# Two rows of w_out split earlier, products with m placed behind the newest half product, m made a step ahead, row writes moved behind m's loads

## The chip, the cores and the metric

The kernel runs on one core of a Trainium2 chip. Time is device microseconds for one execution. The core has TensorE (PE: matrix products; PEld: its weight loads), VectorE (DVE), ScalarE (ACT), GpSimd (POOL) and SyncE (SP), which here issues nearly all transfers. Each engine works through its own instructions in order, and waits at an instruction until what it needs is there.

## The reference

Eight batches of attention between 512 tokens and 32 states in 8 heads, and then a feed-forward block over all rows, whose weights are drawn as 64-bit floats. Below, a is the softmax of the scores over the states, and a2 the same with the states as the queries:

```python
def _attn_ref(x, state):          # x: 8 x 8 x 512 x 64, state: 8 x 8 x 32 x 64
    scores = scale * np.matmul(x, state.transpose(0, 1, 3, 2))
...
    xread = np.matmul(a, state)
...
    sread = np.matmul(a2, x)
    return np.concatenate([xread, sread], axis=2)

def _moe_ref(x, w_in, w_out):     # 4608 rows, w_in 512 x 2048, w_out 2048 x 512
    h = x @ w_in
    g = h - np.tanh(h)
    return g @ w_out
```

## The kernel before

**Chunks and rows.** The tokens of batch i are chunk i (512 rows); the states' rows of all batches are chunk 8 (256 rows). For chunks 0 to 7 the read of the state and the first weight are joined: xread @ w_in is a @ m, where m (256 x 2048 for each batch) is state times w_in, head by head. m is handled in quarters q of 512 columns, and each quarter in two halves k. A hidden product for row f (one of 16 groups of 128 columns of w_in) is `hps`, from `m` and `aT` (the transposed softmax); tanh on ScalarE and a subtraction on VectorE make g. An output product for row f is `ops`, from g and row f of w_out (`wo`), four of them, one for each 128 tokens, added up over the rows in four banks.

**Splitting.** A number is kept as two: a cast to fp32r on ScalarE (the high part) and a subtraction on VectorE (the low part), both in the helper at L103. A product is then three: high with high, high with low, low with high (L501 to L503, L556 to L558). For chunk 0's first half, eight rows (HALT = 8), g and w_out's rows 0 to 7 (PLAIN = 8) stay plain fp32 (tiles `wp`, two rows each) and one fp32 product is used (L499, L554). `split_row` splits those rows later, since the other chunks need them split (`wo`).

**Raw weights.** A block of 64-bit weights is loaded raw, and made fp32 in four steps: two on VectorE, one on ScalarE, one on VectorE (`Weight.steps`, L132 to L136). The raw tiles rotate through six buffers, so a load waits until the block six loads earlier is converted.

**m.** For batches 0 and 1 m is made by `m_first_two` as soon as two blocks of w_in are there (products `mps` at L181, then four copies on ScalarE by `free`). Batch 0's quarters 2 and 3 go to memory (`md02`, `md03`) and are loaded again (`mr02`, `mr03`) by `load_m`, which also splits them (`m02`, `m03`). `mr` is one buffer. For batches 2 to 7 `m_units` makes m from w_in read back and the split states (`sms`, `slr` split to `sls`), stores it (`md` from `st` and `sl`), and `load_m` loads it. Copies out of these banks follow each other in a fixed order, and a new product with m waits until the last of them is done (`behind_free`).

**The order of the work.** A loop over steps `st` goes through `order`: chunk 0's rows 0 to 7, chunk 1's 16 rows, chunk 0's rows 8 to 15, chunks 2 and 3. A step calls, in this order, conversions of weights (tables CONV and WO), `prepare` (which calls `load_m`) where a quarter begins and the hidden product for the row LAG = 2 steps ahead, `split_row` (table SPLITS), `m_first_two` (table PAIRS), side work of other batches, `keep_row` (table KEEP: two writes of a split row of w_out to memory, `wod`, on SyncE) and `mix_rows`, and at last the output products of its own row. A second loop handles chunks 4 to 7 in pairs with the rows read back from `wod` and `wsd`. What stands in which place on an engine is then set by a planner that lists the instructions by its own estimate of when each can start; `tc.issue_after(x)` tells it that what is made inside comes behind x. `keep_row` is told to come behind the last load of raw weights.

Of the kernel before, what the change touches and what calls it, by code (L numbers as in the profile page):

```python
# [27 lines left out]
LAG = 2  # L28
# [1 line left out]
EARLY_S = 2  # L30
LONE = 1
HALT = 8
PLAIN = 8
TURN = (0, 1, 3, 2)


# [1 line left out]
def attention_ffn(ctx: ExitStack, tc: tile.TileContext, xT, xn, bd, bh, sp, sm, sl, win, wout, xout, tout, sout):  # L38
# [10 lines left out]
    nc = tc.nc  # L49
# [28 lines left out]
    mdram = [  # L78
        [dram.tile([2, 4, NS, 512], F32, name=f"md{b}{q}") for q in range(NQ)]
        if b != 1  # L80
        else None
        for b in range(B)
    ]
# [61 lines left out]
    loadlog = []  # L145
# [10 lines left out]
    def second(q):  # L156
        return pool.tile([P, 2, 512], F32, tag="stage", name=f"mr1{q}", bufs=SB)

    def m_first_two(q, p):

        k = p // 2
        if p == 0:

            tag, bufs = ("m", MB) if q == 1 else ("mr", RRB)
            m_first[q] = pool.tile([P, 2, 512], F32, tag=tag, name=f"mr0{q}", bufs=bufs)
            m_second[q] = second(q)
        if p % 2 == 0:
            return
        pss = [bank(ps_a, f"mps0{q}{p - 1 + c}") for c in range(2)]
        run = []  # L170
        for b in range(2):
            for c in (1, 0):
                for e in range(2):
                    r = slice(64 * e, 64 * e + 64)
                    at = 64 * b + 32 * (e ^ c)
                    rows = slice(at, at + 32)
                    with ExitStack() as behind:
                        if run:
                            behind.enter_context(tc.issue_after(run[-1]))
                            behind.enter_context(tc.high_priority())  # L180
                        made = nc.tensor.matmul(  # L181
                            pss[c][rows], sps[r, p - 1 + c, rows], wfs[q, k][r, c], start=True, stop=True
                        )
                    if not run:
                        behind_free(made)
                    run.append(made.ins)
        for c in range(2):
            free(m_first[q][64 * c : 64 * c + 64, k], pss[c][0:64])
            free(m_second[q][64 * c : 64 * c + 64, k], pss[c][64:128])
        if q >= 2 and k:  # L190
            nc.sync.dma_start(mdram[0][q].rearrange("g h n f -> (h n) g f"), m_first[q])

    freed = [None]

    def free(out, src, **more):

# [11 lines left out]
    def m_units():  # L208
# [8 lines left out]
        for q in range(NQ):  # L217
            for k in range(2):
                w = pool.tile([P, 2, 512], F32, tag="wf", name=f"w1{q}{k}", bufs=WB)
                nc.sync.dma_start(w, wf[q][:, 2 * k : 2 * k + 2])  # L220
                for c in range(2):
# [32 lines left out]
                            nc.sync.dma_start(mdram[6 + j][q][k, 2 * c + e], late[rows])  # L254
                    yield

    def load_m(b, q):
        if b == 0 and q < 2:
            return [m_first[q][:, k] for k in range(2)], None
        if b == 1:  # L260
            r = m_second[q]
        else:
            r = pool.tile([P, 2, 512], F32, tag="mr", name=f"mr{b}{q}", bufs=RRB)
            nc.sync.dma_start(r, mdram[b][q].rearrange("g h n f -> (h n) g f"))
        m = pool.tile([P, 2, 2, 512], F32R, tag="m", name=f"m{b}{q}", bufs=MB)
        split(m[:, 0], m[:, 1], r)
        return [m[:, 0, k] for k in range(2)], [m[:, 1, k] for k in range(2)]
# [17 lines left out]
        return his, los  # L285

    def convert_wout(f, part):
        if f < PLAIN:
            if f % 2 == 0:
                plain[f // 2] = big(f"wp{f}", [P, 2, DM], F32)  # L290
            part.convert(plain[f // 2][:, f % 2])
            return
        w = pool.tile([P, 512], F32, tag="c2", name=f"wor{f}", bufs=CSB)
        part.convert(w)
        wo[f] = big(f"wo{f}", [P, 2, DM], F32R)
        split(wo[f][:, 0], wo[f][:, 1], w)


    plain = {}
# [177 lines left out]
    class Chunk:  # L477
# [11 lines left out]
        def hidden(self, f):  # L489

            i, n = self.i, self.n
            ps = bank(ps_h, f"hps{i}_{f}")[:, :n]
            cols = slice((f % 4) * P, (f % 4) * P + P)
            mhi, mlo = self.m[f // 4]
            ahi, alo = aTs[i][:, 0], aTs[i][:, 1]
            nk = 2 if i < B else 4
            for k in range(nk):
                if mlo is None:
                    nc.tensor.matmul(ps, mhi[k][:, cols], ats[k], start=(k == 0), stop=(k == 1))  # L499
                    continue  # L500
                nc.tensor.matmul(ps, mhi[k][:, cols], ahi[:, k], start=(k == 0), stop=False)  # L501
                nc.tensor.matmul(ps, mhi[k][:, cols], alo[:, k], start=False, stop=False)  # L502
                made = nc.tensor.matmul(ps, mlo[k][:, cols], ahi[:, k], start=False, stop=(k == nk - 1))  # L503
                if CL <= i < B:
                    chain[0] = made.ins
            self.finish(f, ps)

        def finish(self, f, ps):
            i, n = self.i, self.n
            t = pool.tile([P, 512], F32, tag="t", name=f"t{i}_{f}", bufs=TB)[:, :n]  # L510
            if CL <= i < B:
                if f % 4 < 2:
                    self.g[f // 4, f % 2] = big(f"G{i}_{f}", [P, 2, 512], F32)
                g = self.g[f // 4, f % 2][:, f % 4 // 2]
                main(nc.scalar.activation(t, ps, AF.Tanh), nc.vector.tensor_sub(g, ps, t))  # L515
                return
            if i == 0 and f < PLAIN:
                g = self.g[f] = pool.tile([P, 512], F32, tag="g", name=f"g{i}_{f}", bufs=GB)
                tanhs.append((nc.scalar.activation(t, ps, AF.Tanh).ins, nc.vector.tensor_sub(g, ps, t).ins))
                return  # L520
            tanhs.append((nc.scalar.activation(t, ps, AF.Tanh).ins, nc.vector.tensor_sub(t, ps, t).ins))  # L521
            g = pool.tile([P, 2, 512], F32R, tag="g", name=f"g{i}_{f}", bufs=GB)
            split(g[:, 0, :n], g[:, 1, :n], t)
            self.g[f] = g
# [23 lines left out]
        def add(self, f, t):  # L548
            g, o = self.g[f], self.o[t]
            tok = slice(t * P, t * P + P)  # L550
            stop = f + 1 in self.begins or f == NFF - 1
            if self.i == 0 and f < PLAIN:
                w = plain[f // 2][:, f % 2]
                return nc.tensor.matmul(o, g[:, tok], w, start=(f in self.begins), stop=stop).ins  # L554
            w = wo[f]
            nc.tensor.matmul(o, g[:, 0, tok], w[:, 0], start=(f in self.begins), stop=False)  # L556
            nc.tensor.matmul(o, g[:, 0, tok], w[:, 1], start=False, stop=False)  # L557
            return nc.tensor.matmul(o, g[:, 1, tok], w[:, 0], start=False, stop=stop).ins  # L558
# [44 lines left out]
    chunks = [Chunk(i) for i in range(B + 1)]  # L603
# [18 lines left out]
            nc.sync.dma_start(wf[q][:, p - 1 : p + 1], wfs[q, p // 2])  # L622


    CONV = [0, 0, 7, 8, 9, 10, 11, 12, 13, 14]
    WO = [0, 1, 2, 3, 4, 5, 6, 8, 9, 10, 12, 13, 14, 15, 16]
    SPLITS = [6 + x for x in range(PLAIN)]
    split_it = iter(range(PLAIN))
    PAIRS = [1, 1, 9, 9, 11, 11, 13, 13, 15, 15]
    rest = w0[1][2:] + w0[2] + w0[3]  # L630
    later = sorted([(s, 0, x) for s, x in zip(CONV, range(10))] + [(s, 1, x) for s, x in zip(WO, range(1, NFF))])
    loads = iter(w0[0] + wos[:1] + w0[1][:2] + [wos[x] if w else rest[x] for _, w, x in later])
# [168 lines left out]
    def keep_row(f):  # L801
        for half in range(2):
            cols = slice(256 * half, 256 * half + 256)
            with tc.issue_after(loadlog[-1]):
                nc.sync.dma_start(wod[:, f % 2, half, f // 2], wo[f][:, :, cols].bitcast(F32))

    def mix_rows(j):
# [38 lines left out]
    order = [(0, f) for f in range(HALT)] + [(1, f) for f in range(NFF)] + [(0, f) for f in range(HALT, NFF)]  # L846
    order += [(i, f) for i in range(2, CL) for f in range(NFF)]
    for st, (i, f) in enumerate(order):
            with ExitStack() as gates:
                for x in tanhs[st - 1] if st > 6 else (first,):  # L850
                    gates.enter_context(tc.issue_after(x))
                for _ in range(CONV.count(st)):
                    convert_win(*next(convs))
                    load(1)
                for _ in range(WO.count(st)):
                    x = next(wo_it)
                    convert_wout(x, wos[x])
                    load(1)
            if st + LAG < len(order):
                ni, nf = order[st + LAG]  # L860
                if nf % 4 == 0:
                    chunks[ni].prepare(nf // 4)
                chunks[ni].hidden(nf)
            with ExitStack() as gates:
                for x in tanhs[max(st - 1, 0)]:
                    gates.enter_context(tc.issue_after(x))
                for _ in range(SPLITS.count(st)):
                    split_row(next(split_it))
            if st in AHEAD:
                x = AHEAD.index(st)  # L870
# [145 lines left out]
    for n, duo in enumerate(duos):  # L1016
        a, b = duo.a.i, duo.b.i
# [5 lines left out]
        for s in range(8):  # L1023
            h = hs[per * s : per * s + per]
# [105 lines left out]
```

## Time and profile before

| what | value |
|---|---|
| median of 3 runs | 659.6 us (659.54 to 662.79) |
| the profiled execution | 660.7 us |
| its span, first to last instruction | 658.9 us |
| PE busy | 637.1 us, 97% |
| PEld, DVE, ACT busy | 485.7, 481.2, 383.3 us |
| DMA | 141.21 MB, mean 214 GB/s |
| granted TensorE clock, mean | 0.997 |

Busy times are sums over the whole span, and a matmul's end is modelled, so PE's 97% says that it rarely waits, not how well each product runs. Lines (L501 and so on) are those of the kernel before. In rows of the trace in order of time, the first number is the start, the second the length; what ended the idle time just before an instruction stands in square brackets. In rows of groups the count follows the x, then the busy time and the mean length in ns, then the idle time before them. A plain fp32 product leaves two records in the trace, a product of fp32r parts one. PEq, SPq and so on are an engine's issuing part.

### The profile page before, as it was taken

The page shows a single profiled execution, that of the slowest core. Times are in us where ns is not written, and L with a number is a line of the kernel's source. Part 1 is how long each engine was busy: PE and PEld are TensorE (multiplying, and loading weights), DVE is VectorE, ACT ScalarE, POOL GpSimd, SP SyncE. Part 2 cuts the span into 40 slices and gives each one's busy share as a digit, 9 for nine tenths or more (in the row PEclk, how much of TensorE's full clock was granted, in tenths as well). Part 3 has the DMA queues.
Part 4 walks back from the last instruction along what each step waited for, and adds up shares of the span by engine and source line. Part 5 has one row for each costly group of instructions (what it writes and reads, how often), then busy time and mean ns, then how long its engine had stood idle before and what let it go on. Part 6 is the DMA issues. An engine that isn't in the chain of part 4 may idle for free.

```text
span 658.9 us, 9567 instructions
## 1 busy us (share of the span) xinstructions
PE 637.1 (97%) x3442; PEld 485.7 (74%) x3442; DVE 481.2 (73%) x764; ACT 383.3 (58%) x666; POOL 26.9 (4%) x41
## 2 busy tenths in 40 slices
PE   5899899999999999999999999999999999999997
PEld 2434477767777778787878887778888888788996
DVE  5887799768557976799637886996965789754442
ACT  3755678667757576576655576355655553543532
POOL 2000000000000000000000000000000000343300
PEclk9899999999999999999999999999999999999999
DMA  9794489997978874644822446464565545899800
GB/s 316 247 366 156 165 289 340 345 320 240 284 243 269 277 254 167 222 161 164 287 96 100 159 125 213 143 203 131 156 186 188 162 129 181 296 324 347 279 8 32
DMA packets 67440, 141.21 MB, mean 214 GB/s; under 512 B 6977, under 2 KB 28737, under 8 KB 67393
## 3 DMA queue, kind: packets, MB, share of 16 engines
q1 hardware_dynamic: 64832, 132.21, 61.0%
q0 software_dynamic: 2560, 8.39, 3.6%
q8 instruction: 27, 0.44, 0.3%
q14 instruction: 21, 0.16, 0.1%
HBM read 96.01 MB, written 44.56 MB: 213 GB/s over the span
## 4 chain that ended last, share of the span: by engine, by line
PE 85%; DVE 8%; DMA 3%; ACT 2%; issue 1%; SPq 0%; ACTq 0%; DVEq 0%
PE X L965 12%; PE hps L501 9%; PE hps L502 9%; PE hps L503 8%; PE ops L556 8%; PE ops L558 8%; PE ops L557 8%; PE Y1m L965 5%; PE ops L554 4%; PE Y0m L965 4%; PE mps L235 2%; PE hps L499 2%; PE mls L242 2%; PE rps L447 1%; PE pps L426 1%
## 5 line engine op out<-in xcount | busy, mean ns | idle before, releaser
L501 PE MATMUL hps<-aT,m 128*128 128x512 f32 x240 | 95.9, 401 | 4.0 <-ACT aT L103 1.6
L502 PE MATMUL hps<-aT,m 128*128 128x512 f32 x240 | 94.0, 392 | 0.0
L503 PE MATMUL hps<-aT,m 128*128 128x512 f32 x240 | 93.4, 391 | 0.0
L556 PE MATMUL ops<-wo,g 128*128 128x512 f32 x224 | 87.3, 395 | 1.6 <-ACT g L103 1.6
L557 PE MATMUL ops<-wo,g 128*128 128x512 f32 x224 | 87.1, 391 | 0.0
L521 DVE TENSOR_TENSOR t<-hps,t 128x512 f32<-128x512 f32 (+1 forms) x72 | 45.1, 627 | 45.8 <-ACT t L521 45.5
L558 PE MATMUL ops<-wo,g 128*128 128x512 f32 x224 | 75.7, 394 | 0.0
L515 ACT ACTIVATE t<-hps 128x512 f32<-128x512 f32 x64 | 38.2, 597 | 63.8 <-PE hps L503 61.5
L515 DVE TENSOR_TENSOR G<-hps,t 128x512 f32<-128x512 f32 x64 | 43.9, 687 | 38.8 <-ACT t L515 38.7
L521 ACT ACTIVATE t<-hps 128x512 f32<-128x512 f32 (+1 forms) x72 | 39.6, 552 | 47.8 <-PE hps L503 46.4
L501 PEld LDWEIGHTS hps<-aT,m 128*128 128x128 f32 x240 | 44.9, 188 | 19.6 <-DVE G L515 3.2
L103 ACT CAST g<-t 128x512 fp32r<-128x512 f32 (+1 forms) x72 | 41.1, 574 | 25.6 <-DVE t L521 25.3
L103 DVE TENSOR_TENSOR g<-t,g 128x512 fp32r<-128x512 f32 (+1 forms) x72 | 45.1, 626 | 13.7 <-ACT g L103 13.4
L502 PEld LDWEIGHTS hps<-aT,m 128*128 128x128 f32 x240 | 45.1, 188 | 10.8 <-issue 1.7
L556 PEld LDWEIGHTS ops<-wo,g 128*128 128x128 f32 x224 | 41.9, 188 | 14.0 <-ACT g L103 2.0
L503 PEld LDWEIGHTS hps<-aT,m 128*128 128x128 f32 x240 | 45.1, 188 | 9.4
L558 PEld LDWEIGHTS ops<-wo,g 128*128 128x128 f32 x224 | 41.7, 188 | 11.5 <-issue 1.2
L557 PEld LDWEIGHTS ops<-wo,g 128*128 128x128 f32 x224 | 42.1, 188 | 9.2 <-issue 0.7
L965 PE MATMUL X<-g0m,W0m 128*128 128x512 f32 x192 | 46.9, 390 | 0.5 <-DVE g0m L103 0.5
L1003 POOL DMA_DIRECT2D wl<-wod x32 | 23.3, 729 | 587.5 <-DVE g1m L103 555.1
L965 PE MATMUL X<-g1m,W1m 128*128 128x512 f32 x192 | 45.9, 391 | 0.6 <-DVE g1m L103 0.6
L103 ACT CAST g1m<-G 128x1024 fp32r<-128x1024 f32 x28 | 29.3, 1055 | 28.8 <-PE Y1m L965 12.7
(262 smaller groups left out, 1182.0 us busy)
## 6 DMA issues: line engine op xcount, KB each, us to landing
mr<-md SPq DMA_DIRECT2D x26, 512.0 KB, 3.9
xT<-in_xT SPq DMA_DIRECT2D x16, 512.0 KB, 4.9
wod<-wo SPq DMA_DIRECT2D x32, 256.0 KB, 5.3
md<-st SPq DMA_DIRECT2D x64, 128.0 KB, 3.1
xn<-in_xn SPq DMA_DIRECT2D x16, 512.0 KB, 5.0
wsd<-ws SPq DMA_DIRECT2D x16, 512.0 KB, 3.5
W0m<-wsd SPq DMA_DIRECT2D x16, 512.0 KB, 4.0
W1m<-wsd SPq DMA_DIRECT2D x16, 512.0 KB, 4.3
```

The source lines that it names most:

```text
L103: return nc.scalar.copy(hi, src), (sub or nc.vector).tensor_sub(lo, src, hi)
L501: nc.tensor.matmul(ps, mhi[k][:, cols], ahi[:, k], start=(k == 0), stop=False)
L502: nc.tensor.matmul(ps, mhi[k][:, cols], alo[:, k], start=False, stop=False)
L503: made = nc.tensor.matmul(ps, mlo[k][:, cols], ahi[:, k], start=False, stop=(k == nk - 1))
L515: main(nc.scalar.activation(t, ps, AF.Tanh), nc.vector.tensor_sub(g, ps, t))
L521: tanhs.append((nc.scalar.activation(t, ps, AF.Tanh).ins, nc.vector.tensor_sub(t, ps, t).ins))
L554: return nc.tensor.matmul(o, g[:, tok], w, start=(f in self.begins), stop=stop).ins
L556: nc.tensor.matmul(o, g[:, 0, tok], w[:, 0], start=(f in self.begins), stop=False)
L557: nc.tensor.matmul(o, g[:, 0, tok], w[:, 1], start=False, stop=False)
L558: return nc.tensor.matmul(o, g[:, 1, tok], w[:, 0], start=False, stop=stop).ins
L965: made = nc.tensor.matmul(out[t], w[:, e, x, cols], y[:, e], start=first and j == 0 and e == 0 and c == 0, stop=last and j == 3 and e == 1 ...
L1003: nc.gpsimd.dma_start(wo[f][:, :, cols].bitcast(F32), wod[:, f % 2, half, f // 2])
```

## The change

Six things are done. Rows 2 and 3 of w_out are split at once when they are converted, and chunk 0 uses them with a split g, three products for one; rows 0, 1, 4, 5, 6 and 7 stay plain. The tables of steps shift by one for some conversions and splits, row 8's conversion among them. The first product of a group with m comes behind the newest split hidden product. `prepare` for a new quarter is called a step sooner. `keep_row` comes behind the newest load of m, not behind the last load of raw weights. Apart from the three products for one in rows 2 and 3, the same is computed.

```diff
-PLAIN = 8
+PLAIN = (0, 1, 4, 5, 6, 7)
...
                         if run:
                             behind.enter_context(tc.issue_after(run[-1]))
                             behind.enter_context(tc.high_priority())
+                        elif newest[0] is not None:
+                            behind.enter_context(tc.issue_after(newest[0]))
...
-            nc.sync.dma_start(r, mdram[b][q].rearrange("g h n f -> (h n) g f"))
+            lastmr[0] = nc.sync.dma_start(r, mdram[b][q].rearrange("g h n f -> (h n) g f")).ins
...
-        if f < PLAIN:
-            if f % 2 == 0:
+        if f in PLAIN:
+            if f // 2 not in plain:
                 plain[f // 2] = big(f"wp{f}", [P, 2, DM], F32)
...
                 made = nc.tensor.matmul(ps, mlo[k][:, cols], ahi[:, k], start=False, stop=(k == nk - 1))
+                newest[0] = made.ins
...
-            if i == 0 and f < PLAIN:
+            if i == 0 and f in PLAIN:
...
-    SPLITS = [6 + x for x in range(PLAIN)]
+    SPLITS = [6,7,10,11,12,13]
...
-            with tc.issue_after(loadlog[-1]):
+            with tc.issue_after(lastmr[0]):
                 nc.sync.dma_start(wod[:, f % 2, half, f // 2], wo[f][:, :, cols].bitcast(F32))
...
-                if nf % 4 == 0:
+                if nf // 4 not in chunks[ni].m:
                     chunks[ni].prepare(nf // 4)
                 chunks[ni].hidden(nf)
+                if st + LAG + 1 < len(order):
+                    ni, nf = order[st + LAG + 1]
+                    if nf % 4 == 0 and st > 1:
+                        chunks[ni].prepare(nf // 4)
```

Three places show what the planner makes of it. The first is ScalarE where chunk 1 begins (`aT1` from `at11`: the second half of chunk 1's aT; `t1_0`: tanh of its first row; `mr02`, `mr12`: copies of a product with m). Before:

```order
L103 CAST aT1_336<-at10_447 128x512
L579 COPY ob0_21_565<-ops0_0_2_345 128x512
L200 COPY mr02_657<-mps020_659 64x512
L200 COPY mr12_658<-mps020_659 64x512
L200 COPY mr02_657<-mps021_660 64x512
L200 COPY mr12_658<-mps021_660 64x512
L103 CAST aT1_336<-at11_474 128x512
L521 ACTIVATE t1_0_518<-hps1_0_511 128x512
```

Now:

```order
L103 CAST aT1_338<-at11_501 128x512
L585 COPY ob0_21_584<-ops0_0_2_347 128x512
L527 ACTIVATE t1_0_545<-hps1_0_538 128x512
L135 ACTIVATE w22r_636<-w22d_487 128x512
L527 ACTIVATE t1_1_565<-hps1_1_558 128x512
L135 ACTIVATE wo8r_644<-wo8d_515 128x512
L135 ACTIVATE w23r_698<-w23d_536 128x512
L103 CAST g1_0_548<-t1_0_545 128x512
L103 CAST g1_1_568<-t1_1_565 128x512
L527 ACTIVATE t1_2_613<-hps1_2_606 128x512
L527 ACTIVATE t1_3_661<-hps1_3_654 128x512
L203 COPY mr02_670<-mps020_672 64x512
```

The four copies of the product with m stood ahead of the cast of aT's second half, and now stand behind chunk 1's fourth tanh.

The second is SyncE's queue where m of batch 0 is stored and loaded again (`wod`: writes of rows; `slr`: states for the last two batches). Before:

```order
L191 DMA md03_84<-mr03_866 128x2x512
L805 DMA wod_77<-wo13_906 128x2x256 x2
L215 DMA slr_1045<-in_sl 128x512
L220 DMA w101_1191<-wf0_110 128x1024
L805 DMA wod_77<-wo14_943 128x2x256 x2
L220 DMA w110_1338<-wf1_111 128x1024
L250 DMA md20_85<-st00_1069 32x2x512
L250 DMA md30_89<-st00_1069 32x2x512
L250 DMA md40_93<-st00_1069 32x2x512
L250 DMA md50_97<-st00_1069 32x2x512
L264 DMA mr02_1311<-md02_83 128x2x512
```

Now:

```order
L223 DMA w101_1212<-wf0_110 128x1024
L193 DMA md03_84<-mr03_890 128x2x512
L269 DMA mr02_1320<-md02_83 128x2x512
L218 DMA slr_1069<-in_sl 128x512
L223 DMA w110_1359<-wf1_111 128x1024
L253 DMA md20_85<-st00_1093 32x2x512
```

The load of m02 follows the store of md03 at once, and the row writes are gone from here; the first of them now stands behind the load `mr20`, ten of them ahead of the loads of chunk 0's partial sums (`part`).

The third is ScalarE some ten rows later, around the split of slr (`sls`) and of m02. Before:

```order
L103 CAST wo15_992<-wor15_986 128x512
L521 ACTIVATE t1_11_1027<-hps1_11_1020 128x512
L103 CAST g1_10_1005<-t1_10_1002 128x512
L200 COPY st00_1069<-mps00_1055 128x512
L200 COPY st00_1069<-mps01_1056 128x512
L103 CAST g1_11_1030<-t1_11_1027 128x512
L103 CAST sls_1046<-slr_1045 128x512
```

Now:

```order
L103 CAST wo15_1013<-wor15_1007 128x512
L103 CAST sls_1070<-slr_1069 128x512
L103 CAST g1_10_1026<-t1_10_1023 128x512
L527 ACTIVATE t1_11_1048<-hps1_11_1041 128x512
L103 CAST m02_1322<-mr02_1320 128x1024
L203 COPY st00_1093<-mps00_1079 128x512
L203 COPY st00_1093<-mps01_1080 128x512
L103 CAST g1_11_1051<-t1_11_1048 128x512
```

The casts of sls and of m02 came behind g of row 11 (m02's nine rows behind it), and now stand ahead of it.

More of the change, by code (lines that the diff above doesn't have):

```diff
@@ L193, in attention_ffn @@
     freed = [None]
+    newest = [None]
     def free(out, src, **more):
@@ L255, in m_units @@
                     yield
+    lastmr = [None]
     def load_m(b, q):
@@ L551, in add @@
             stop = f + 1 in self.begins or f == NFF - 1
-            if self.i == 0 and f < PLAIN:
+            if self.i == 0 and f in PLAIN:
                 w = plain[f // 2][:, f % 2]
@@ L622, in convert_win @@
             nc.sync.dma_start(wf[q][:, p - 1 : p + 1], wfs[q, p // 2])
-    CONV = [0, 0, 7, 8, 9, 10, 11, 12, 13, 14]
-    WO = [0, 1, 2, 3, 4, 5, 6, 8, 9, 10, 12, 13, 14, 15, 16]
-    SPLITS = [6 + x for x in range(PLAIN)]
-    split_it = iter(range(PLAIN))
+    CONV = [0, 0, 8, 8, 9, 10, 11, 12, 13, 14]
+    WO = [0, 1, 2, 3, 4, 5, 6, 9, 10, 11, 12, 13, 14, 15, 16]
+    SPLITS = [6,7,10,11,12,13]
+    split_it = iter(PLAIN)
     PAIRS = [1, 1, 9, 9, 11, 11, 13, 13, 15, 15]
```

## The prediction

> **What bounds the kernel now.** I read the busy time by stage first, then the list of TensorE's waits, then the chain of waits, and last the engines in order of time around each wait. The stages (start and end, length, then busy time and count of PE, PEld, DVE, ACT, POOL, the granted clock, DMA share, GB/s):
>
> ```profile
> 72.00:82.00 10.00, 7.42 (x42) 4.59 (x27) 5.99 (x12) 7.22 (x13) 0.00 (x0) 1.00 0.33 125
> 82.00:125.00 43.00, 43.00 (x224) 32.28 (x223) 43.00 (x74) 35.60 (x62) 0.00 (x0) 1.00 0.96 331
> 125.00:140.00 15.00, 13.41 (x69) 8.85 (x68) 8.15 (x13) 7.49 (x14) 0.00 (x0) 1.00 0.99 331
> ...
> 200.00:400.00 200.00, 199.89 (x1304) 157.64 (x1303) 153.08 (x278) 126.17 (x237) 0.00 (x0) 1.00 0.56 187
> ...
> PE ops L556 <- ACT g L103: 1.6, 1, 1.6
> PE hps L501 <- ACT aT L103: 1.6, 1, 1.6
> PE hps L501 <- DVE t L521: 1.0, 1, 1.0
> ```
>
> TensorE is the bound: 199.89 of 200 us busy in the long middle stage. Time can be won only by taking work off it, or at its idle spots: 2.58 us between 72 and 82, and 1.59 between 125 and 140, which are the three waits listed. From 82 to 125 VectorE has no idle time either, so a stage that starts sooner must also get its VectorE work sooner.
>
> The chain shows how those spots arise (start, length, what):
>
> ```profile
> 48.25 3.43 PE ops L554 x8
> ...
> 71.79 1.10 PE mps L181 x16
> ...
> 72.91 0.58 ACT mr L200
> ...
> 75.29 0.63 ACT aT L103
> ...
> 75.96 0.73 PE hps L501 x2
> ...
> 78.15 0.70 DVE t L521
> ...
> 78.89 0.50 PE hps L501
> ...
> 83.73 0.91 PE ops L558 x4
> ```
>
> **The split of rows 2 and 3.** Four plain fp32 products of one row of w_out (eight records) take 3.43 us. Split they are twelve, at 0.91 / 4 = 0.2275 each: 2.73. Two rows save 2 x 0.70 = 1.40 us of TensorE work, with no cover over it, since TensorE runs back to back there.
>
> [...]
>
> What is added is one cast and one subtraction of g for each row; the split of the weights itself only comes earlier.
>
> ```profile
> L103 ACT CAST g<-t 128x512 fp32r<-128x512 f32 (+1 forms) x72 | 41.1, 574 | 25.6 <-DVE t L521 25.3
> ...
> L103 DVE TENSOR_TENSOR g<-t,g 128x512 fp32r<-128x512 f32 (+1 forms) x72 | 45.1, 626 | 13.7 <-ACT g L103 13.4
> ...
> 39.45 0.69 ACT L135 ACTIVATE wo5r<-wo5d 128x512 int32<-128x512 uint32 x1 [3.80 <-DMA wo5d<-in_wout]
> ...
> 46.03 1.23 DVE L103 TENSOR_TENSOR m<-mr,m 128x1024 fp32r<-128x1024 f32 x1 [1.67 <-ACT m L103]
> ```
>
> That is 1.15 us of ScalarE and 1.25 of VectorE, hidden by the idle 3.80 and 1.67. The tight place is the low part of g for row 3. ScalarE is held for row 5's raw weights until 39.45 in both kernels; counting the new order on from there at the same steps, m10 is cast by 43.9, row 3 by 44.4, g by 45.5, and VectorE subtracts g at 47.9 to 48.5. TensorE's last four products of row 3 come at about 48.9. A miss costs its own length: 0 to 0.7 us, taken as 0.
>
> **The products with m behind the newest half product.** Before, the four copies of a product with m stood on ScalarE ahead of the cast of the second half of chunk 1's aT, so that cast waited for TensorE's product (end 72.89) and four times 0.58: it ran at 75.29. Now the copies stand behind chunk 1's fourth tanh. The cast then waits for the transpose of that half on VectorE:
>
> ```profile
> 63.79 0.42 DVE L132 TENSOR_SCALAR wor<-wo8d 128x512 uint32<-128x512 uint32 x1
> ...
> 70.94 0.68 DVE L103 TENSOR_TENSOR wo<-wp,wo 128x512 fp32r<-128x512 f32 x1
> ...
> 72.74 0.71 DVE L380 STREAM_TRANSPOSE at<-e 128x512 f32<-128x512 f32 x1
> ```
>
> Ahead of the transpose there no longer stand row 8's three conversion steps and its subtraction (0.33 + 3 x 0.6, start to start), row 2's subtraction (0.6) and the two copies of the output (1.2): 3.9 us less. With the 1.4 us from above it comes at 72.74 - 3.9 - 1.4 = 67.4, the cast near 68.7, the low part near 69.7. TensorE reaches chunk 1 at 71.79 - 1.4 = 70.4 and finds aT there. From 71.79 to 78.89 it spends 7.10 us now: 1.10 on m, 12 x 0.2275 = 2.73 on the first two half products, and 3.27 on waits and restarts. The wait for a bank of hps that tanh and subtraction hand back, 1.0 as listed, stays with its restart, about 1.1. **So 2.2 us go**; lower bound 1.57, the listed wait, upper bound 3.27. The product with m itself is only moved: it waits behind the fourth half product, where its weights are ready.
>
> What is late next: row 8's conversion, now behind 78 in old times, adds 2.1 us to the stage in which VectorE is full. VectorE begins that stage with chunk 1's first subtraction, 78.15 before, about 73.3 now (70.4, ten products 2.3, a tanh 0.6), 5 us sooner, so it still leaves it some 2.5 sooner. TensorE comes 3.6 sooner; counted row by row along the new order, VectorE keeps 1 to 2 us in hand at every half product up to row 9. I take nothing for it; without that cover it costs up to 1.1.
>
> **m a step ahead, row writes behind m's loads.** These rows carry the second idle spot:
>
> ```profile
> 118.52 1.22 DVE L103 TENSOR_TENSOR m<-mr,m 128x1024 fp32r<-128x1024 f32 x1
> ...
> 113.19 2.38 ACT L200 COPY mr<-mps 64x512 f32<-64x512 f32 x4
> ...
> 121.77 0.67 SPq L191 DMA_DIRECT2D md<-mr  x1
> ...
> 124.57 0.72 SPq L215 DMA_DIRECT2D slr<-in_sl  x1
> ...
> 131.92 0.38 SPq L264 DMA_DIRECT2D mr<-md  x1
> ...
> 129.28 0.62 ACT L103 CAST sls<-slr 128x512 fp32r<-128x512 f32 x1 [4.08 <-DMA slr<-in_sl]
> ...
> 137.14 1.04 ACT L103 CAST m<-mr 128x1024 fp32r<-128x1024 f32 x1 [1.88 <-DMA mr<-md]
> ...
> 138.76 0.50 PE L556 MATMUL ops<-wo,g 128*128 128x512 f32 x1 [1.59 <-ACT g L103]
> ...
> mr<-md SPq DMA_DIRECT2D x26, 512.0 KB, 3.9
> ...
> md<-mr SPq DMA_DIRECT2D x2, 512.0 KB, 4.2
> ...
> slr<-in_sl SPq DMA_DIRECT2D x1, 256.0 KB, 4.7
> ...
> 124.74 0.39 PE L556 MATMUL ops<-wo,g 128*128 128x512 f32 x1
> ```
>
> The load of m02 leaves SyncE at 131.92, six us behind the row writes and what they hold up; ScalarE stands 1.88 us at its cast with the cast of g behind it, and TensorE waits 1.59 for that g. Now md03 leaves when its copies are done (115.6 before, near 112), lands 4.2 later, and m02 is loaded by about 120. **1.59 us go.**
>
> **The wait that takes its place.** The new order puts the cast of sls ahead of g for row 10 on ScalarE, and two products with sls ahead of row 10 on TensorE. slr needs a buffer that m13's subtraction frees: 119.74 before, now 2.4 sooner (5 sooner less the 2.6 us more work), so it leaves at 117.4 and lands 4.7 later at worst, or 3.5 (the fastest load of mr in the trace's view of that tile); I take the middle, 121.5, and 122.1 with the cast. TensorE is there at 124.74 - 3.6 = 121.1 and waits 1.0. Behind sls stand g, a tanh, m02's cast and two copies (0.52 + 0.5 + 1.0 + 1.0) before the bank for chunk 2's scores is free at 125.1; TensorE asks for it at 124.7. **So 1.5 us are given back**, 0.9 at the fast landing, 2.1 at the slow one.
>
> **The row writes' new place.** 32 issues leave the stretch from 97 to 134 and go between 151 and 265, past the stores and loads of m:
>
> ```profile
> L805 SPq DMA_DIRECT2D wod<-wo x32: 359/668/2102, 97.2 to 133.4; - x32
> ...
> 195.37 3.29 SPq L563 DMA_DIRECT2D part<-halfd  x4
> ...
> 205.60 1.28 DVE L577 TENSOR_TENSOR ob<-ops,part 128x512 f32<-128x512 f32 x2
> ...
> 207.42 0.40 PE L556 MATMUL ops<-wo,g 128*128 128x512 f32 x1
> ...
> 312.81 1.60 SPq L914 DMA_DIRECT2D W0m<-wod  x1
> ...
> part<-halfd SPq DMA_DIRECT2D x4, 256.0 KB, 3.5
> ```
>
> Ten stand ahead of chunk 0's partial sums: 10 x 0.668 = 6.7 us on a queue that hardly rests there. The first such load would leave at 195.37 - 3.7 + 6.7 = 198.4 and land at 201.9; its addition comes at 205.60 - 3.7 = 201.9. It fits to the tenth; the writes' shortest issue (0.359) leaves 3 us, the mean of the crowded stretch more than 0.8 would miss. Priced at 0, with the miss as a rival. Nothing reads the written rows before 312.81.
>
> **The sum**: -1.40 - 2.2 - 1.59 + 1.5 = -3.7 us. From the profiled execution's 660.7 (span 658.9 and 1.8 around it) that is 657.0; the median of the runs is 659.6, 1.1 below it, which gives **655.9 us**.
>
> **The rivals.**
> 1. slr is there in time (0.12). For: the row writes are gone from the DMA engines, which stood at 0.99 busy. Against: 3.5 is the fastest load seen. Then nothing is given back: 655.9 - 1.5 = 654.4. [...]
> 2. sls and VectorE together (0.18): slr lands at the slow end (+0.6) and the full VectorE stage takes its 1.1. For: VectorE's 43.00 of 43. Against: TensorE was never held there before. 655.9 + 1.7 = 657.6.
> 3. The change does not do what it says (0.10): the idle spots return elsewhere before 140, and only the 1.40 of TensorE work stays. For: ScalarE and VectorE keep one order each, and the new one has waits as well. Against: the aT cast has no long wait left. 659.6 - 1.4 = 658.2.
> 4. Slower (0.10): SyncE's queue becomes the bound at 195. If each write costs 1.2 us there (between the median and the longest, 2.102), ten cost 12; the partial sum lands at 207.2 instead of 201.9, its two banks are handed back 5.3 us late, and TensorE, which opens chunk 2's outputs 0.5 us behind the two additions (206.88 to 207.42), waits for 4.8. 655.9 + 4.8 = 660.7. It decides from 0.7 us for each write. For: the queue has some 130 more issues of m's parts around it. Against: the long issues fell where the DMA engines were full.
>
> **How the numbers follow.** My forecast has 0.50. With the miss at row 3 and the bounds of the aT term (1.57 to 3.27) its own range is 654.3 to 657.2. What a measurement here can tell from no change is about 0.5%, 3.3 us: faster means below 656.3. Of the forecast I put 0.40 below that, 0.10 above; rival 1 is below. Faster 0.52; same 0.42 (0.10, rivals 2 and 3, and 0.04 of rival 4, which starts inside the band); slower 0.06. The range 653.8 to 659.4 takes in the first three rivals and leaves out the fourth and the edges.
>
> **What would show each step.** Split: rows 2 and 3 as twelve products each, 2.73 a row, and no wait ahead of the last four of row 3. aT: the wait of 1.57 before chunk 1 is gone and the one of 1.0 behind it stays. m02: no cast waits for its load, and no wait of row 12's product for g. In its place a wait of TensorE for ScalarE's cast of sls at about 121. SyncE: the partial sums' load within 3 us of 195 and no wait of TensorE near 204. The prediction is wrong if TensorE's waits between 70 and 140 add up to more than 4 us, or if a new one stands behind 200.

## The result, and the profile after

| | before | changed |
|---|---|---|
| median | 661.1 us (6 runs on the same chip) | 668.7 us |
| ratio, with its 95% interval | 1 | 1.0102 (1.008 to 1.0125) |
| the profiled execution | 660.7 us | 669.0 us |
| its span | 658.9 us | 667.2 us |
| granted TensorE clock, mean | 0.997 | 0.991 |

The change makes the kernel 1% slower; 655.9 us was forecast. One of its six executions took 2234.92 us; the median counts it, the ratio does not. The stages of the changed kernel, as in the first view of the prediction:

```profile
72.00:82.00 10.00, 8.98 (x51) 6.16 (x50) 7.72 (x15) 6.88 (x13) 0.00 (x0) 1.00 0.55 183
125.00:140.00 15.00, 15.00 (x81) 10.70 (x81) 8.04 (x13) 9.36 (x17) 0.00 (x0) 1.00 0.81 243
...
205.00:225.00 20.00, 16.88 (x80) 10.43 (x79) 11.39 (x20) 8.97 (x17) 0.00 (x0) 0.91 0.83 267
225.00:270.00 45.00, 39.96 (x239) 30.78 (x238) 30.65 (x61) 26.36 (x51) 0.00 (x0) 0.96 0.99 325
```

Up to 140 all went as forecast or better: TensorE (the first busy time) is idle for 1.02 us between 72 and 82 instead of 2.58, and not at all between 125 and 140. But behind 205, where it had no idle time before, it stands for 3.12 and 5.04 us, at a granted clock of 0.91 and 0.96. The same two stretches before:

```profile
205.00:225.00 20.00, 20.00 (x103) 14.06 (x102) 17.21 (x34) 13.60 (x28) 0.00 (x0) 1.00 0.77 231
225.00:270.00 45.00, 45.00 (x327) 36.03 (x326) 34.67 (x65) 29.48 (x59) 0.00 (x0) 1.00 0.70 240
```

The last two columns belong to it: from 225 to 270 the DMA engines went from 0.70 to 0.99 busy, and from 240 to 325 GB/s.

To see where the time goes I take the starts of the same instructions in both traces and compare the lengths between them: from the first output product (30.8 before) to chunk 1's scores (53.3), to chunk 1's fifth hidden product (87.2), to the one that stands at 201.4, and so on. The table has the difference to the kernel before, in us; the executions start up to 2 us apart, and this leaves that out. All the kernels that were run are in it, to be used below.

| kernel | 31 to 53 | 53 to 87 | 87 to 201 | 201 to 224 | 224 to 251 | 251 to 279 | 279 to 647 |
|---|---|---|---|---|---|---|---|
| the change | -1.35 | -2.11 | -2.23 | +5.12 | +1.51 | +5.96 | +0.27 |
| rows back | -1.36 | -2.10 | +6.09 | 0.00 | +0.48 | 0.00 | +0.05 |
| rows alone | +1.09 | -0.01 | -2.23 | +6.48 | +1.30 | +6.85 | +0.24 |
| ten back | -0.10 | -2.07 | +1.60 | 0.00 | +1.50 | +2.60 | +0.02 |
| rows by GpSimd | -1.37 | -2.10 | -2.23 | +3.12 | +0.71 | +5.16 | +1.85 |
| rows late | -1.34 | -2.11 | -2.23 | 0.00 | +0.43 | -0.01 | +0.07 |
| small writes | -0.72 | -2.10 | -2.22 | +0.71 | +0.31 | +2.77 | +0.06 |
| before, rows late | +0.12 | +0.04 | -2.22 | -0.01 | +0.01 | -0.01 | +0.08 |
| rows late, no split | +0.22 | -0.57 | -1.80 | 0.00 | +0.01 | -0.01 | +0.10 |
| rows late, m as before | -1.35 | +0.76 | -1.80 | 0.00 | 0.00 | 0.00 | +0.03 |
| rows late, no step ahead | -0.53 | -2.07 | -2.22 | 0.00 | +0.33 | +0.38 | +0.05 |

The change wins 5.7 us up to 201 and loses 12.6 between 201 and 279. TensorE's waits in the lost stretch, then ScalarE's (engine, line, what it waited for; in all, times, longest):

```profile
PE sps L345 <- ACT st L203: 2.6, 1, 2.6
PE pps L431 <- ACT sr L203: 2.5, 1, 2.5
PE hps L506 <- DVE t L527: 2.1, 2, 1.4
...
ACT m L103 <- DMA mr<-md: 8.8, 2, 6.5
ACT st L203 <- DMA md<-st: 3.8, 1, 3.8
ACT sl L247 <- DMA md<-sl: 3.7, 2, 2.3
```

TensorE waits for ScalarE; ScalarE waits for transfers of m. Before, its wait for `mr` was 3.6 in two, the longest 2.0, and it never waited for `md<-st`. The queue of SyncE in the two places, in order of time:

```profile
192.49 2.41 SPq L811 DMA_DIRECT2D wod<-wo  x3
194.99 1.95 SPq L253 DMA_DIRECT2D md<-st  x4
197.04 1.77 SPq L257 DMA_DIRECT2D md<-sl  x4
198.85 1.40 SPq L569 DMA_DIRECT2D part<-halfd  x3
...
202.40 2.23 SPq L253 DMA_DIRECT2D md<-st  x2
...
249.30 0.95 SPq L269 DMA_DIRECT2D mr<-md  x1
250.31 6.49 SPq L811 DMA_DIRECT2D wod<-wo  x8
```

and ScalarE beside it:

```profile
196.96 1.08 ACT L203 COPY st<-mps 128x512 f32<-128x512 f32 x2 [1.10 <-PE mps L238]
...
202.89 1.08 ACT L203 COPY st<-mps 128x512 f32<-128x512 f32 x2
...
211.31 1.07 ACT L203 COPY st<-mps 128x512 f32<-128x512 f32 x2 [3.84 <-DMA md<-st]
...
255.81 1.05 ACT L103 CAST m<-mr 128x1024 fp32r<-128x1024 f32 x1 [6.52 <-DMA mr<-md]
```

The copies of 196.96 fill one of the two stage buffers and are done at 198.0. Their store leaves at 202.40, 4.4 us later, behind the row writes, the partial sums and what else had queued up; the last of its four parts (two are issued behind the lines shown) lands at 211.13, and at 211.31 ScalarE fills that buffer again. TensorE's next scores (`sps`, line 345) wait for a bank that those copies hand back. In the second place m23 is loaded at 249.30 (241.57 before), with eight row writes issued right behind it and the DMA engines full (a busy share of 1.03 from 249.3 to 255.8), and lands 6.5 us later; ScalarE stands at its cast, with a tanh and the copies `sr` queued behind it. The landings from 180 to 270 (issues, KB each, median us from issue to landing), before:

```profile
md<-st SPq DMA_DIRECT2D x32, 128.0 KB, 2.6
...
mr<-md SPq DMA_DIRECT2D x4, 512.0 KB, 4.5
```

and changed:

```profile
wod<-wo SPq DMA_DIRECT2D x28, 256.0 KB, 5.5
md<-st SPq DMA_DIRECT2D x32, 128.0 KB, 3.4
...
mr<-md SPq DMA_DIRECT2D x4, 512.0 KB, 5.4
```

These two waits of TensorE cost more than their length. The sixteen products of the scores behind the first wait take 1.96 us, where they took 1.09 before:

```profile
212.43 1.96 PE L345 MATMUL sps<-xT,bdr 64*32 64x512 f32 x16 [2.58 <-ACT st L203]
```

These are TensorE's products behind the second (start, length):

```profile
262.33 1.16 PE L431 MATMUL pps<-ident,s 128*128 128x128 f32 x8 [2.49 <-ACT sr L203]
263.17 0.74 PE L508 MATMUL hps<-aT,m 128*128 128x512 f32 x1
263.71 0.63 PE L506 MATMUL hps<-aT,m 128*128 128x512 f32 x1
264.14 0.63 PE L507 MATMUL hps<-aT,m 128*128 128x512 f32 x1
...
266.27 0.57 PE L562 MATMUL ops<-wo,g 128*128 128x512 f32 x1
266.68 0.40 PE L563 MATMUL ops<-wo,g 128*128 128x512 f32 x1
266.92 0.40 PE L564 MATMUL ops<-wo,g 128*128 128x512 f32 x1
```

They start 0.43 us apart until 266.68, and 0.23 apart from then on. Eight products take the 3.5 us from 263.17 to 266.68, where 8 x 0.23 = 1.8 would do: 1.7 us on top of a wait of 2.5. The granted clock is 0.50 from 212.0 to 215.4 and from 263.2 to 266.6, and 1.00 between and around them.

### The profile page after: what moved, and what is told of

Its sections match the earlier page's. It is cut to its first block, busy times and chain, and to the rows that moved or that the text cites. A ratio compares the mean times of both kernels' runs of the same rounds, so it can differ in the third digit from the quotient of the medians.

```text
span 667.2 us, 9583 instructions
## 1 busy us (share of the span) xinstructions
PE 640.7 (96%) x3450; PEld 489.4 (73%) x3450; DVE 482.0 (72%) x766; ACT 384.8 (58%) x668; POOL 27.0 (4%) x41
## 4 chain that ended last, share of the span: by engine, by line
PE 82%; DVE 8%; DMA 5%; ACT 3%; issue 1%; SPq 1%; ACTq 0%; DVEq 0%
PE X L975 12%; PE ops L562 8%; PE hps L506 8%; PE ops L563 8%; PE ops L564 8%; PE hps L508 8%; PE hps L507 8%; PE Y1m L975 5%; PE Y0m L975 3%; PE ops L560 3%; DMA mr<-md 2%; PE hps L504 2%; PE mps L238 2%; PE mls L245 1%; DMA w01d<-in_win 1%
## 5 line engine op out<-in xcount | busy, mean ns | idle before, releaser
L562 PE MATMUL ops<-wo,g 128*128 128x512 f32 x232 | 91.1, 400 | 0.3 <-DVE ob L583 0.3
L563 PE MATMUL ops<-wo,g 128*128 128x512 f32 x232 | 89.9, 392 | 0.0
L527 DVE TENSOR_TENSOR t<-hps,t 128x512 f32<-128x512 f32 (+1 forms) x74 | 46.5, 629 | 49.4 <-ACT t L527 49.0
L564 PE MATMUL ops<-wo,g 128*128 128x512 f32 x232 | 82.0, 396 | 0.0
L506 PEld LDWEIGHTS hps<-aT,m 128*128 128x128 f32 x240 | 45.2, 188 | 21.1 <-DVE t L527 4.2
L562 PEld LDWEIGHTS ops<-wo,g 128*128 128x128 f32 x232 | 43.7, 189 | 16.2 <-issue 3.1
L564 PEld LDWEIGHTS ops<-wo,g 128*128 128x128 f32 x232 | 43.7, 189 | 12.4 <-DVE wst L103 1.7
L563 PEld LDWEIGHTS ops<-wo,g 128*128 128x128 f32 x232 | 43.8, 189 | 10.3 <-issue 1.2
```

## The experiments

### Are the row writes the loss at all? Rows back, and rows alone

```diff
 rows back: the changed kernel, keep_row
-            with tc.issue_after(lastmr[0]):
+            with tc.issue_after(loadlog[-1]):
```

> The changed kernel with one thing undone: the row writes come behind the last load of raw weights again, as before. Theory Q (the row writes cost on SyncE's queue and on the DMA engines behind 150, and cost all that is lost): no wait of TensorE between 207 and 223 nor between 243 and 266, where the changed kernel lost 12.7 us against the one before; the 4.6 us that it was ahead at 207 stay, less up to 1.6 if the load of m02 is late again behind the row writes: 656.5 to 658 against 661.1 before. Rival T (TensorE, 4.6 us sooner, asks for m's buffers sooner than its stores can free them, row writes or not): the two stalls stay, 665 or more.

Measured 663.2 us, ratio to before 1.0033 (1.0013 to 1.0052). The two stalls behind 201 are gone, as theory Q said, but the time is not: 6.09 us are lost between 87 and 201.

```profile
129.36 0.72 PE L245 MATMUL mls<-wst,sls 128*128 128x512 f32 x2 [1.02 <-ACT sls L103]
...
135.96 1.65 PE L245 MATMUL mls<-wst,sls 128*128 128x512 f32 x3 [4.25 <-ACT sl L247]
```

These are TensorE's waits there. `slr` is issued at 122.79 between row writes and lands 5.9 us later (116.46 and 3.7 in the changed kernel). The new order of TensorE asks for sls ahead of row 10, where the kernel before asked later, and now stands. So the rest of the change can't have the rows in their old place either; I had expected 1.6 us at most.

```diff
 rows alone: the kernel before, load_m and keep_row
-            nc.sync.dma_start(r, mdram[b][q].rearrange("g h n f -> (h n) g f"))
+            lastmr[0] = nc.sync.dma_start(r, mdram[b][q].rearrange("g h n f -> (h n) g f")).ins
...
-            with tc.issue_after(loadlog[-1]):
+            with tc.issue_after(lastmr[0]):
```

> The kernel before with the move of the row writes alone. Theory Q: the same issues stand in the same stretches of SyncE's queue, so the same stalls arise: up to 12.7 us more than before, less 1.6 for a load of m02 in time, and less where the stores have slack because TensorE comes 4.6 us later: 666 to 672. Rival T: row writes cost nothing while TensorE isn't ahead, 659.5 to 661.5.

Measured 672.4 us, ratio 1.0174 (1.0127 to 1.0221). Rival T falls: by the table TensorE is only 1.2 us ahead here at 201 (5.7 in the change), and the stalls are larger (+6.48, +1.30, +6.85). The row writes do it, and their leaving 97 to 134 is what wins the 2.23 us between 87 and 201.

```profile
207.78 0.47 PE L558 MATMUL ops<-wo,g 128*128 128x512 f32 x1 [2.01 <-DVE ob L579]
...
216.88 1.09 PE L342 MATMUL sps<-xT,bdr 64*32 64x512 f32 x16 [1.87 <-ACT st L200]
```

The first of these waits is the prediction's fourth rival, a bank held by a late partial sum. In the changed kernel that addition came only 0.56 us late.

### Which writes make which stall? Ten back

```diff
 the changed kernel, keep_row
-            with tc.issue_after(lastmr[0]):
+            with tc.issue_after(loadlog[-1] if f < 5 else lastmr[0]):
```

> The changed kernel with the first ten row writes (rows 0 to 4) back behind the last load of raw weights, the other 22 left behind the loads of m. Theory Q in its two places: the ten make the first stall (5.1 us lost between 207 and 223), the 22 the second (6.0 us between 243 and 266, and 1.0 between): 668.7 - 5.1 = 663.6, with the wait for the stage buffer at 212 gone and the one behind the load of m23 at 259 still there. Rival T: 667 or more, both stalls there. If the second stall only follows from the first one: 656 to 658.

Measured 664.5 us, ratio 1.0048 (1.002 to 1.0075). The first stall belongs to the ten writes: without them 201 to 224 is as before. The second stays with the other 22, at 1.50 + 2.60 us instead of 1.51 + 5.96: its wait of 2.37 has no half rate behind it (more in the last section), and the wait of 1.37 ahead of it is not there. Even ten writes in the old place cost: TensorE waits 1.90 us for sls at 124, at half rate behind it, and 87 to 201 is 1.60 longer than before instead of 2.23 shorter.

### Issues or bytes? Rows by GpSimd, and small writes

A row write could do the harm here in two ways: its issue takes time on SyncE's queue (0.55 us at the median), ahead of m's stores and loads, or its 256 KB take time of the DMA engines (0.99 busy from 225 to 270) from theirs.

```diff
 the changed kernel, keep_row
-            with tc.issue_after(lastmr[0]):
-                nc.sync.dma_start(wod[:, f % 2, half, f // 2], wo[f][:, :, cols].bitcast(F32))
+            made = nc.gpsimd.dma_start(wod[:, f % 2, half, f // 2], wo[f][:, :, cols].bitcast(F32))
+            info = mybir.DependencyInfo(mybir.DependencyClass.Sync, mybir.DependencyReason.DATA)
+            tc.add_manual_dep(made.ins, lastmr[0].name, info, reason="newest load of m")
```

> The changed kernel with the row writes issued by GpSimd, each waiting for the same load of m that it stood behind on SyncE: the bytes move in about the same stretches, but take no time on SyncE's queue. Theory Q1 (SyncE's queue: an issue of 0.36 to 1.3 us, 32 of them, ahead of m's stores and loads): 656 to 658. Theory Q2 (the DMA engines are full there, 0.9 to 1.1 busy; m's stores and loads share them with 8 MB of rows): 665 to 669, loads of m still landing 5.5 to 6.5 us after their issue instead of 4.5.

Measured 665.6 us, ratio 1.0079 (1.0051 to 1.0108): the bytes without SyncE's time keep 10.8 of the 12.9 us behind 201. ScalarE's wait for m23, and the landings of `mr` from 195 to 275:

```profile
250.67 1.05 ACT L103 CAST m<-mr 128x1024 fp32r<-128x1024 f32 x1 [5.74 <-DMA mr<-md]
```

```profile
DMA to landing us min/median/max: 4.7/5.6/8.7
```

Here m23 left SyncE in time, at 241.94, and landed 8.7 us later, beside five row writes that GpSimd issued between 235 and 241. So another queue took away about a sixth of the loss (2.0 of 12.9 us).

The counterpart has the issues without the bytes. It builds on the kernel with the late rows (next section), and adds small writes in the places of the changed kernel's row writes:

```diff
+    def small_row(f):
+        for half in range(2):
+            with tc.issue_after(lastmr[0]):
+                nc.sync.dma_start(small[2 * f + half], wo[f][0:2, 0, 0:128].bitcast(F32))
...
+                if 32 <= st < 48:
+                    small_row(st - 32)
```

> The kernel with the late rows, and in the places in which the changed kernel has its 32 row writes on SyncE's queue, 32 writes of 1 KB each from the same tiles into memory that nothing reads: the issue times without the bytes. Theory Q1 (the issues themselves, ahead of m's stores and loads): the stall near 212 and the one near 259 are back, 5 us or more above the kernel with the late rows. Theory Q2 (the bytes: m's stores and loads wait behind the rows' data on the DMA engines): within 1 us of the kernel with the late rows. The run with the rows on GpSimd's queue kept 3.0 of the 5.1 us and 5.2 of the 7.0, so Q2 should have most of it: 0 to 2.5 us.

Measured 658.9 us, ratio 0.996 (0.9937 to 0.9983), 3.4 us above the late rows: more than the 2.5 that I allowed for Q2. By place: +0.71 at the first stall (5.12 with the whole rows), -0.12 against the late rows from 224 to 251, +2.78 behind. TensorE's waits:

```profile
252.56 1.10 PE L433 MATMUL pps<-ident,s 128*128 128x128 f32 x8 [0.76 <-ACT sr L204]
272.26 1.09 PE L347 MATMUL sps<-xT,bdr 64*32 64x512 f32 x16 [1.68 <-DMA xT<-in_xT]
```

The first is the second stall's own wait at 0.76 instead of 2.49. The second is for a load that stands behind late row writes and small writes together, and belongs to neither of the changed kernel's stalls. Behind 201 this run loses 3.3 us more than the late rows; without that load, the issues make under 2 us of the 12.9. They are shorter than those that they stand for, though: 0.25 us at the median and 10.3 in all, where the changed kernel's row writes took 0.55 and 21.1. That the bytes make most of the loss therefore rests on the run with GpSimd, and bytes are not told apart there from the number of packets that carry them. The two runs do not add up exactly, since each also shifts what it meets.

The bytes hold up SyncE's queue here too. Counted from the first output product, the store for which the first stall waits leaves 4.3 us later in the changed kernel than with the late rows of the next section, and still 3.2 later with the rows by GpSimd. With the late rows its four parts also take 6.7 to 7.1 us to land (5.9 to 7.7 in the change), so at the first stall the store is late because it leaves late. At the second, m23 also takes longer: it lands 5.4 us after its issue with the late rows, 6.5 in the change, 8.7 with GpSimd.

### A place that costs nothing: rows late

```diff
 the changed kernel
-    KEEP = [32 + x for x in range(16)]
+    KEEP = [45 + x * 9 // 16 for x in range(16)] + [54 + x * 10 // 16 for x in range(16)]
...
-    def keep_row(f):
-        for half in range(2):
-            cols = slice(256 * half, 256 * half + 256)
-            with tc.issue_after(lastmr[0]):
-                nc.sync.dma_start(wod[:, f % 2, half, f // 2], wo[f][:, :, cols].bitcast(F32))
+    def keep_row(f, half):
+        cols = slice(256 * half, 256 * half + 256)
+        with tc.issue_after(anchor[0]):
+            nc.sync.dma_start(wod[:, f % 2, half, f // 2], wo[f][:, :, cols].bitcast(F32))
```

`anchor` is the newest load of m or store to `wsd`; half 0 of all rows goes first, even rows ahead of odd ones.

> The changed kernel with all 32 row writes behind the load of m30 (at 250 in the kernel before) or later, each behind the newest load of m or store of a mixed row, half 0 of the rows first: out of 97 to 134 and out of 150 to 250. Theory Q (the rest of the change gains as predicted, the rows took it back): no wait of TensorE for the stage buffer near 212 nor for sr near 259, TensorE stays 4.6 us ahead of the kernel before: 655 to 657.5 where before stands at 660.7. Rival R (wherever the 8 MB of rows go behind 150, they cost some 5 us, as with GpSimd): 661 or more, with a new wait between 260 and 345.

Measured 655.5 us, ratio 0.9906 (0.9875 to 0.9936): 0.9% faster than the kernel before, and, by the two ratios, 1.9% faster than the change. TensorE's list of waits has nothing between 75 and 400:

```profile
74.42 0.50 PE L506 MATMUL hps<-aT,m 128*128 128x512 f32 x1 [1.02 <-DVE t L527]
402.31 1.09 PE L345 MATMUL sps<-xT,bdr 64*32 64x512 f32 x16 [0.54 <-ACT sr L203]
```

The bytes are the same 8.4 MB. They now run where there is room, and TensorE hardly feels them:

```profile
205.00:225.00 20.00, 20.00 (x104) 14.27 (x103) 16.71 (x34) 12.54 (x25) 0.00 (x0) 1.00 0.83 263
225.00:270.00 45.00, 44.90 (x335) 35.31 (x334) 32.55 (x58) 29.38 (x58) 0.00 (x0) 1.00 0.87 295
270.00:345.00 75.00, 75.00 (x541) 59.93 (x540) 55.31 (x111) 46.83 (x94) 0.00 (x0) 1.00 0.73 248
```

Rival R falls; only 0.5 us is lost behind 201, nearly all of it from 224 to 251.

### What each other part is worth

> The kernel before with its row writes moved as in the kernel with the late rows, and nothing else of the change. Theory Q: the load of m02 is in time, the idle 1.59 at 138 is gone as it was with the row writes moved alone (2.2 ahead at 131), and nothing is lost later: 658 to 659.5 where before stands at 660.7. What the kernel with the late rows gains beyond this is the split of rows 2 and 3 and the product with m moved: 1.4 + 2.2 predicted, less 1.5 given back. Rival R: 662 or more.

The kernel before, with `keep_row`, `KEEP` and `anchor` as in the last diff: 659.2 us, ratio 0.9969 (0.995 to 0.9989). The place of the rows alone is worth 1.8 us by the medians and 2.0 by the table, all of it won between 87 and 201 (2.22); the wait of 1.58 for aT at 75 is still there.

```diff
 rows late, no split
-PLAIN = (0, 1, 4, 5, 6, 7)
+PLAIN = tuple(range(8))
...
-    CONV = [0, 0, 8, 8, 9, 10, 11, 12, 13, 14]
-    WO = [0, 1, 2, 3, 4, 5, 6, 9, 10, 11, 12, 13, 14, 15, 16]
-    SPLITS = [6,7,10,11,12,13]
+    CONV = [0, 0, 7, 8, 9, 10, 11, 12, 13, 14]
+    WO = [0, 1, 2, 3, 4, 5, 6, 8, 9, 10, 12, 13, 14, 15, 16]
+    SPLITS = [6 + x for x in range(8)]
```

> The kernel with the late rows, with w_out's rows 2 and 3 plain again in chunk 0 (and the tables of steps as before): one part of the change undone. By the term of the prediction 1.40 us slower than the kernel with the late rows (its traces show 21.23 us from the first plain output product to chunk 1's scores, against 22.57 before: 1.34). So 656.8 where the late rows give 655.4 and before 661.0, if the time that the split saves is not won back at a later wait. If the rows' place is all that mattered, no difference.

Measured 658.4 us, ratio 0.9961 (0.9943 to 0.9979), 2.9 us above the late rows: twice the forecast. The products account for 1.56 of it (+0.22 instead of -1.34). The tables add 1.54: row 8's conversion stands ahead of the transpose on VectorE again (72.34, against 67.93 in the late rows), and TensorE waits again for aT:

```profile
73.74 0.73 PE L506 MATMUL hps<-aT,m 128*128 128x512 f32 x2 [0.67 <-ACT aT L103]
```

```diff
 rows late, m as before
-                        elif newest[0] is not None:
-                            behind.enter_context(tc.issue_after(newest[0]))
```

> The kernel with the late rows, with the products with m of batches 0 and 1 no longer told to come behind the newest half product: the other part undone. By the term of the prediction (the cast of aT stands again behind four copies of such a product) 2.2 us slower than the late rows: 657.6, with the wait of about 1.6 for aT back near 71. If another wait of VectorE's full stage behind it takes over anyway, less than 1 us slower.

Measured 657.1 us, ratio 0.9953 (0.9936 to 0.997), 1.7 us above the late rows. In the profiled execution (658.8) the stretch from 53 to 87 is 2.87 longer than with the late rows, a little more than the 2.2 of the term, but by another wait than I named:

```profile
77.16 0.50 PE L504 MATMUL hps<-aT,m 128*128 128x512 f32 x1 [2.28 <-DVE t L525]
77.49 0.39 PE L505 MATMUL hps<-aT,m 128*128 128x512 f32 x1
77.72 0.58 PE L506 MATMUL hps<-aT,m 128*128 128x512 f32 x1
78.11 0.63 PE L504 MATMUL hps<-aT,m 128*128 128x512 f32 x1
```

aT is in time, because the tables made the transpose early. The four copies now stand ahead of chunk 1's first tanh instead, so the bank of hps comes 1.26 us later than with the late rows (2.28 against 1.02), and the half rate follows. It does not in every execution: two of the six, the profiled one among them, had a mean granted clock of 0.995 and took 658.8 us; the other four had 0.997, as the late rows have, and took 656.4 to 657.6.

```diff
 rows late, no step ahead
-                if st + LAG + 1 < len(order):
-                    ni, nf = order[st + LAG + 1]
-                    if nf % 4 == 0 and st > 1:
-                        chunks[ni].prepare(nf // 4)
```

> The kernel with the late rows, with m's quarters prepared at their own step again and not one ahead. The kernel before with late rows had no wait for m02 without this, so the step ahead has nothing to gain there: within 1 us of the kernel with the late rows. If the step ahead is what frees TensorE at 138, it is 1.6 us slower.

Measured 655.3 us, ratio 0.9923 (0.9907 to 0.9939): as the late rows. m a step ahead is worth nothing here that can be told from the noise.

## Why the prediction was wrong

The step that failed is "The row writes' new place", priced at 0. Its check of the queue was right where it looked: the loads of the partial sums were to leave at 198.4 and left at 198.85, and their addition came 0.56 us late. It looked at one reader only. The same ten writes stood ahead of m's stores, and a store that is late holds one of two stage buffers; 22 more stood among the loads of m22, m23 and m30, of which the prediction says only that the writes go past m's stores and loads and that nothing reads the written rows before 312.81. And it counted the issues on SyncE's queue only, where the cost was mainly bytes on DMA engines that were at 0.70 to 0.77 before. At 0 the step missed 12.6 us. The sign that the prediction itself names, a new wait behind 200, is what came.

The "fourth rival" had the right place, SyncE's queue at 195, and the wrong victim: its 4.8 us through the partial sums occurred as a wait of 2.01, in the run with the rows alone. Its chance of 0.10 was too small because only one consumer was followed.

The other terms, against the table:

- Split of rows 2 and 3: -1.40 forecast, -1.35 measured. The tight place at the low part of g was missed in three runs (ten back, small writes, no step ahead), by a wait of 0.34 or 0.35 us between 49 and 50; these are the three whose first stretch lost part of the 1.35.
- The cast of aT: -2.2 forecast, -2.11 measured, and the wait of 1.02 for the bank stayed as said. The prediction gave one sum for two causes; the runs show that each is needed: with only the tables undone 1.54 of it goes, with only the place of m undone all of it and 0.76 more (in the profiled execution, which had the half rate).
- m02: -1.59 forecast, -2.23 measured from 87 to 201, all of it by the rows' place.
- The wait that takes its place: +1.5 forecast, nothing measured. slr left at 116.46, a microsecond ahead of the estimate, landed at the fast end (3.7 us), and its cast ran at 120.23 without a wait. This is the first rival. Its argument against, that 3.5 is the fastest load seen, holds for mr alone: the load of wo11d, 512 KB, landed after 3.24 in the kernel before.
- The range: its lower end, 654.3, is not what the bounds named for it give (655.9 - 1.07 = 654.8).

Up to 201 the sum was thus -5.7 instead of -3.7, and the kernel with the rows out of the way confirms it: 655.5 us where before measured 661.1 beside it, 5.6 less. That this is near the 655.9 forecast for the change itself is chance: the forecast started from 659.6.

What stays open: the share of bytes and issues at the second stall can't be split exactly, because in the run with the small writes a load of xT that is late for both adds 1.68 and the small issues are shorter than the rows' own.

## What to carry to other kernels

When a batch of transfers moves to another place, list every transfer that is in flight in that stretch, with what its lateness holds up: not only the loads that a product reads, but the stores whose landing hands a buffer back. Look at the share of the DMA engines there as well as at the queue: here GpSimd as the issuer left 10.8 of the 12.9 us, in stretches where SyncE's issues had the engines 0.83 to 0.99 busy, and behind the load of m30 the same bytes cost 0.5 us. Where two changes lean on each other, as here the early casts of sls and m02 on the absence of the rows, undo them one at a time before either is judged.

## What the runs showed of the chip

Several waits of TensorE cost more than their length. Behind those of 2.58 and 2.49 us (the change), 1.90 (ten back), 2.28 (rows late, m as before) and 4.25 (rows back) the granted clock was 0.50 and the products ran at about half rate (128x512 products 0.43 us apart instead of 0.23 in the change), for 3.41 us, or twice that behind 4.25. Behind waits of 1.59 (before), 1.87 and 2.01 (rows alone) and 2.37 (ten back) they did not.

The length of the wait alone did not decide it: 1.90 had the half rate behind it and 2.37 had not. In the trace of the changed kernel the granted clock changes at 27.70, 31.11, 212.02, 215.43, 263.22, 266.63 and 665.99, and in that of the kernel before at 26.74, 30.15 and 658.21, in each trace whole multiples of 3.413 us apart. Cut into stretches of this length, the two traces have the clock at 0.50 behind stretches with 2.06 us idle on TensorE or more (2.06 and 3.04 before, 2.07, 2.16, 2.49 and 2.53 in the change) and at 1.00 behind all others, of which the longest idle is 1.82 us (before). In the run with ten back the wait of 2.37 fell on two such stretches, with 1.31 and 1.06 us idle in them, and the wait of 1.90 into one. So where a wait fell counted too. Executions of one kernel differed as well: with m as before two of six ran at a mean clock of 0.995 and took 658.8 us, the other four at 0.997 and 656.4 to 657.6.
